# Masked keys written straight from PSUM, two first LayerNorm sums on ScalarE, and a replayed instruction plan with other constants

## The chip, the cores and the metric

The kernel runs on one core of a Trainium2 chip. The core has a matrix engine (TensorE, PE in the profile, with its weight loads as PEld), a vector engine (VectorE, DVE), a scalar engine (ScalarE, ACT), a small general engine (GpSimd, POOL) and a queue engine that issues most transfers (SyncE, SP). Each runs its own list of instructions in order and waits on semaphores for the others. Matmul results land in PSUM, which is divided into eight banks; everything else lies in SBUF.

The metric is the device time of one execution in microseconds (us). The time before is 551.91 us, the median of five runs (551.07 to 553.73).

## The reference

Two layers, each a sliding-window attention and a gated feed-forward block, over a sequence of 2048 with 512 features. Both layers use the same weights.

```python
def _A_ref(x, wqkv, wo):
    H = 32; Dh = D // H; W = 256
    qkv = ... (x @ wqkv) ...                      # q, k, v: 32 heads of 16
    scores = jnp.einsum("bhqd,bhkd->bhqk", q, k) * (Dh ** -0.5)
    mask = (idx[:, None] - idx[None, :] >= 0) & (idx[:, None] - idx[None, :] < W)
    p = _softmax(jnp.where(mask[None, None], scores, -1e9), axis=-1)
    o = jnp.einsum("bhqk,bhkd->bhqd", p, v)
    return ... o ... @ wo

def _B_ref(x, w_gate, w_up, w_down):              # 512 -> 1792 -> 512
    h = _sigmoid(x @ w_gate) * (x @ w_up)
    return h @ w_down

x = x + _A_ref(_layernorm(x, axis=-1), A_wqkv, A_wo)
x = x + _B_ref(_layernorm(x, axis=-1), B_w_gate, B_w_up, B_w_down)
...
return x
```

The two lines are done twice. LayerNorm has no weights: subtract the mean, divide by the root of the variance plus 1e-5.

## The kernel before

**Tiling.** The sequence is 16 tiles of 128 rows; four tiles make a group. The residual `xsb` stays in SBUF for the whole kernel. Every step of the network is cut into small units, and units of attention, of the projections and of the feed-forward block, of different tiles and both layers, are interleaved on TensorE. A PSUM tile `Sps` of four banks holds the scores of one visit; the other four banks are given to units in turn.

**The units.** For each tile: LayerNorm (`layer_norm`, L489), with the sums on VectorE (L498, L499), the root on GpSimd (L503, L504), the normalisation on VectorE (L520), and a transpose, for the first tiles on TensorE (L532, copied out by the helper at L553 and L555), for the others by a transfer on SP (L544). For each group: four q units (L572) and four k units (L601), and a v unit for each tile (L637). The keys are needed twice, in two copies that have every other 16 rows set to zero, since a head has only 16 features and a row group of TensorE holds two heads. So a k unit copies its bank to `kt` (ScalarE or VectorE), and VectorE then multiplies it with two 0/1 columns, `rms[0]` and `rms[1]`, into the two halves of `kTp` (L615). Then come the scores (visits "A", "R" and "S", L853 to L873), exp on ScalarE from `Sps` into `PTring` or `edge` (L905), the masks on VectorE (L791), the values (L932), a copy to `OTs`, two transposes by transfers with the normalisation of the softmax between them (L951, L986, L987, L959), and the output projection (L723) with its addition to `xsb` (L729). The feed-forward block has gate and up matmuls (L662), tanh on ScalarE (L674; a sigmoid is half of one plus tanh of the half), a multiplication on VectorE (L677), and the down matmuls (L695) with their addition (L704).

**The order.** No loop nest sets the order. A planner (`Plan`, L168) simulates the five engines with a clock of its own while the kernel is being built. It gives each instruction a cost in nanoseconds, each task a priority (a lower number goes first), and, whenever an engine is free in its clock, emits the best task that is ready; `pick` (L1029) does so for TensorE. What comes out is a fixed list for each engine. So a changed cost or priority changes the lists of all engines from that point on, also where no operation changes. Where TensorE has nothing ready in the planner's clock and it is before 85 us, the planner emits four dummy matmuls of the identity (`keep_warm`, L1108, instructions at L1112), which compute nothing that is used. The planner's matmul costs are doubled until `COLD` (L102, L283):

```python
    def matmul(self, mode, ns):
        if self.now < COLD:
            ns *= 2
        if self.mode != mode:
            ns += SWITCH
```

Feed-forward units take two tiles at a time (matmuls 256 wide), and one tile at a time (128 wide) for the first four tiles and the last four (L1285). The functions that the change touches:

Of the kernel before, what the change touches and what calls it, by code (L numbers as in the profile page):

```python
# [13 lines left out]
P = 128  # L14
# [65 lines left out]
def act_ns(n):  # L80
    return 171 + n / 1.2


def dve_ns(n):
    return 152 + n / 0.96
# [15 lines left out]
PE_LATENCY = 180  # L101
COLD = 13600  # L102
SWITCH = 96
# [195 lines left out]
class Net:  # L299
# [189 lines left out]
    def layer_norm(self, key, t, deps, prio):  # L489
# [11 lines left out]
        def root(e):  # L501
            st = box["st"][0]
            nc.gpsimd.tensor_scalar(out=st[:, 9:10], in0=st[:, 7:8], scalar1=1e-5, scalar2=None, op0=ALU.add)  # L503
            nc.gpsimd.tensor_tensor(out=st[:, 8:9], in0=st[:, 9:10], in1=self.nhalf[:], op=ALU.pow)  # L504
# [10 lines left out]
        def apply(e):  # L515
            box["xn"] = b = self.take("xn")
            if key not in self.xnT:
                self.xnT[key] = self.take("xnT")
            st = box["st"][0]
            nc.vector.tensor_scalar(out=b[0][:], in0=self.xsb[:, t, :], scalar1=st[:, 6:7], scalar2=st[:, 8:9],  # L520
                                    op0=ALU.subtract, op1=ALU.mult)

        a = pl.task({"DVE": 910}, stats, deps, prio, lambda: self.has("st"))
        b = pl.task({"POOL": 800}, root, [a.done], prio)
# [68 lines left out]
    def k_unit(self, L, g, cq):  # L593
# [10 lines left out]

        def evac(u):
            box = {}
            u.done.then(lambda: self.used(key, 1))

            def cp(e):
                box["kt"] = self.take("kt")  # L610
                self.copy(e, box["kt"][0][:], self.banks[u.bank][:])

            def split(e):
                for i in range(2):
                    nc.vector.tensor_scalar(out=self.kTp[gi % 2][:, cq, :, i, :], in0=box["kt"][0][:].rearrange("p (t k) -> p t k", k=P),  # L615
                                            scalar1=self.rms[i][:, 0:1], scalar2=None, op0=ALU.mult)

            a = pl.task({"ACT": act_ns(TGW), "DVE": dve_ns(TGW)}, cp, [u.done], 2, lambda: self.has("kt"))
            b = pl.task({"DVE": 620}, split, [a.done], 2, port=True)
            b.done.then(lambda: (self.give(box["kt"]), self.k_ready[L, g, cq].fire()))  # L620
            return a.done
# [3 lines left out]
        if gi >= 2:  # L625
            needs.append(self.seen[divmod(4 * (gi - 2) + 3, NT)])
        u = Unit(("k", L, g, cq), steps, needs, False, evac)
        if by_tile:
# [61 lines left out]
    def down_unit(self, L, t, t0, n, chunks):  # L690
# [12 lines left out]
        def evac(u):  # L703
# [3 lines left out]
            if L == 0:  # L707
                self.layer_norm(("p", 1, t // NBG), t, [d.done], 3)
            else:
                dst = self.out[0, t * P:(t + 1) * P, :].rearrange("(z k) d -> z k d", z=2)  # L710
                for z in range(2):
                    pl.dma(450, HP * D * 2, lambda z=z: nc.sync.dma_start(out=dst[z], in_=self.xsb[z:P:2, t, :]), [d.done])
# [6 lines left out]
    def oproj_unit(self, L, t, b):  # L719
# [7 lines left out]
        def evac(u):  # L727
            u.done.then(lambda: self.give(b))
            d = pl.task({"DVE": dve_ns(D)}, lambda e: nc.vector.tensor_tensor(  # L729
                out=self.xsb[:, t, :], in0=self.xsb[:, t, :], in1=self.banks[u.bank][:], op=ALU.add), [u.done], 1)  # L730
            self.layer_norm(("g", L, t // NBG), t, [d.done], 1 if L * NT + t < 4 else 2)
            return d.done
# [33 lines left out]
    def visit_exp(self, s):  # L766
# [14 lines left out]
        def job(h, what):  # L781
# [6 lines left out]
            if what == "m2":  # L788
# [3 lines left out]
                out=r, in0=r, in1=m.to_broadcast([P, 16, HP]), op=ALU.mult), [x.done, self.has_mask],  # L792
                {"m0": 2, "e0": 2, "e1": 6, "m2": 6}[what], port=True).done
            for hh in ((0, 1) if what[0] == "e" else (h,)):
# [38 lines left out]
    def scores(self, L, t, kind, i):  # L833
# [5 lines left out]
        if kind == "A":  # L839
# [9 lines left out]
            for e in range(2):  # L849
                for k, pos, n in runs:  # L850
                    q0, o = t * P + (k + 1) * HP, e * w + pos * HP
                    for m in range(4):
                        nc.tensor.matmul(self.sps[:, m, o:o + n * HP], lhsT=kTp[32 * m:32 * m + 32, i, tt, e, :],  # L853
                                         rhs=self.qT[32 * m:32 * m + 32, i, q0:q0 + n * HP],
                                         start=True, stop=True, tile_position=(32 * m, 0))
            return pl.count(8 * len(runs)) or 220
        if kind == "R":
            zs = range(2 if t + 2 < NT else 1)
            for z in zs:
                for cq in range(NCQ):  # L860
                    q0, o = t * P + 5 * z * HP, (z * NCQ + cq) * HP
                    for m in range(4):
# [3 lines left out]
                                         start=True, stop=True, tile_position=(32 * m, 0))  # L866
            return pl.count(16 * len(zs)) or 122 * len(zs)
        for cq in range(NCQ):
# [38 lines left out]
    def values(self, L, t, half, bank):  # L907
# [7 lines left out]
        for col in range(4):  # L915
# [10 lines left out]
            for k, (where, Va, p) in enumerate(parts):  # L926
# [8 lines left out]
                pl.count(4)  # L935
        return n * 56

    def after_values(self, L, t, half, bank, done):
# [21 lines left out]

        a = pl.task({"DVE": dve_ns(512), "ACT": act_ns(512)}, move, [done], 0 if early else 1, lambda: "OTs" in box or self.has("OTs"))
        box[half] = a.done
# [3 lines left out]
        if self.by_pe(L, t):  # L966
            self.turn_by_pe(L, t, box)
            return
        b = pl.dma(1800, 262144, turn, [box[0], box[1]], 0 if early else 1)
        b.can = lambda: self.has("Oq")  # L970
        b.done.then(lambda: self.give(box["OTs"]))
        c = pl.task({"DVE": 960}, norm, [b.done], 0 if early else 2, lambda: self.has("On"), port=True)
        c.done.then(lambda: (self.give(box["Oq"]), self.give(box["Rt"])))
        d = pl.dma(1190, 131072, turn2, [c.done], 0 if early else 1)
        d.can = lambda: self.has("OnT")
# [258 lines left out]
    def go(self, *srcs):  # L1234
# [47 lines left out]
        for L in range(2):  # L1282
            t0 = 0
            while t0 < NT:
                k = 1 if L * NT + t0 < 4 or L * NT + t0 >= 2 * NT - 4 else 2  # L1285
                m = FC * k // 2
# [59 lines left out]
```

## Time and profile before

| what | value |
|---|---|
| five runs | 551.07 to 553.73 us, median 551.91 |
| profiled execution | 551.91 us, of which its span is 550.2 us |
| POOL busy, share of the span | 61.9 us, 11% |
| exp on ScalarE (L905), `PTring` and `edge` | 154 instructions, 282.5 us |
| gate and up matmuls, 256 wide / 128 wide | 1344 / 896 |
| down, output projection, q, k, v matmuls, 512 wide | 448, 128, 124, 124, 128 |
| dummy matmuls (L1112) | 84, from 1.4 to 58.1 us |
| first scores (L853) on TensorE | 13.79 us |

The page gives the busy time of each engine, and groups of equal instructions with their count, their sum and the mean time of one. Matmuls are pipelined: one of 128 columns is shown with 219 ns, but the next starts 56 ns later, so a cost on TensorE is read from the distance of starts in the timeline and not from the length of one instruction. "Idle before, releaser" says how long an engine had nothing to do ahead of an instruction, and what ended it; "issue" stands for waits that the profile can't put down to another engine or transfer. The timeline gives start, duration, engine, line, operation and tiles, with equal neighbours merged into one row (x12).

### The profile page before, as it was taken

To read this page: it belongs to the slowest core of one execution; us is meant where nothing else is said; L and a number is where in the kernel's file an instruction comes from. 1 tells how busy PE (TensorE), PEld (TensorE's weight loads), DVE (VectorE), ACT (ScalarE), POOL (GpSimd) and SP (SyncE) were. 2 spreads that over 40 slices of the span, in tenths; PEclk is the share of its full clock that TensorE was granted. 3 is DMA by queue.
4 is the path that set the end of the run, shared out by engine and by line. 5 is a ranking of instruction groups with operands and counts; after the bars stand their busy time and mean duration, and the time that the engine had idled before them with its cause. 6 is when DMAs were issued, how large, how long until landed. Compare 5 with 4: busy or idle time off the path is not lost.

```text
span 550.2 us, 24339 instructions
## 1 busy us (share of the span) xinstructions
PE 526.9 (96%) x10953; PEld 355.3 (65%) x11052; DVE 413.1 (75%) x901; ACT 398.4 (72%) x464; POOL 61.9 (11%) x145
## 2 busy tenths in 40 slices
PE   7999999999999999999999999999999999989996
PEld 6547757757667566666566664666756766667883
DVE  6999898697799698789675795867766677756442
ACT  3998889889889788677687875878768777643320
POOL 5212110020011120002010120100000000000000
PEclk9999999999999999999999999999999999999999
DMA  8694423153223332125201252013520142222000
GB/s 275 210 177 141 61 47 57 31 64 70 43 58 63 71 42 61 32 56 94 49 14 30 52 89 62 17 37 69 90 70 13 41 85 57 50 50 54 17 21 29
DMA packets 97016, 36.43 MB, mean 66 GB/s; under 512 B 79248, under 2 KB 96912, under 8 KB 96912
## 3 DMA queue, kind: packets, MB, share of 16 engines
q1 hardware_dynamic: 95040, 33.04, 28.3%
q8 instruction: 86, 1.41, 1.0%
q10 hardware_dynamic: 1872, 1.84, 1.0%
q14 instruction: 18, 0.15, 0.1%
HBM read 9.70 MB, written 2.10 MB: 21 GB/s over the span
## 4 chain that ended last, share of the span: by engine, by line
PE 88%; issue 3%; DMA 3%; ACT 3%; DVE 2%; SPq 0%; ACTq 0%; DVEq 0%
PE bank L662 34%; PE bank L695 16%; PE bank L932 8%; PE Sps L853 7%; PE bank L601 5%; PE bank L572 5%; PE bank L723 5%; PE bank L637 5%; DMA OnT<-On 2%; ACT PTring L905 2%; PE Sps L863 2%; DMA xnT<-xn 1%; DVE st L498 0%; DVE xn L520 0%; PE bank L532 0%
## 5 line engine op out<-in xcount | busy, mean ns | idle before, releaser
L905 ACT ACTIVATE PTring<-Sps 128x2048 bf16<-128x2048 f32 (+1 forms) x122 | 225.8, 1851 | 49.5 <-PE Sps L853 47.1
L662 PE MATMUL bank<-xnT,wu 128*128 128x256 bf16 (+1 forms) x1120 | 139.8, 251 | 0.7 <-issue 0.7
L662 PE MATMUL bank<-xnT,wg 128*128 128x256 bf16 (+1 forms) x1120 | 139.0, 252 | 0.2
L677 DVE SCALAR_TENSOR_TENSOR hT<-th,bank 128x256 bf16<-128x256 bf16 x224 | 87.8, 414 | 40.8 <-ACT th L674 39.8
L674 ACT ACTIVATE th<-bank 128x256 bf16<-128x256 f32 x224 | 81.0, 385 | 51.0 <-PE bank L662 48.1
L695 PE MATMUL bank<-wd,hT 128*128 128x512 bf16 x395 | 104.5, 379 | 3.3 <-issue 1.4
L662 PEld LDWEIGHTS <-wg 128*128 128x128 bf16 x1120 | 90.4, 98 | 26.5 <-issue 2.2
L662 PEld LDWEIGHTS <-wu 128*128 128x128 bf16 x1120 | 92.0, 98 | 12.3 <-issue 1.6
L503 POOL TENSOR_SCALAR st<-st 128x1 f32<-128x1 f32 x64 | 19.4, 303 | 442.3 <-DVE st L499 442.3
L791 DVE TENSOR_TENSOR PTring<-PTring,mask 128x1024 bf16<-128x1024 bf16 x64 | 44.0, 687 | 30.8 <-ACT PTring L905 30.5
L905 ACT ACTIVATE edge<-Sps 128x2048 bf16<-128x2048 f32 (+1 forms) x32 | 56.7, 1773 | 12.8 <-PE Sps L863 12.8
L695 PEld LDWEIGHTS <-hT 128*128 128x128 bf16 x448 | 40.8, 98 | 32.1 <-issue 0.6
L932 PE MATMUL bank<-PTring,Vaug 128*32 128x64 bf16 (+1 forms) x2880 | 52.1, 203 | 0.5 <-issue 0.5
L853 PE MATMUL Sps<-qT,kTp 32*128 32x64 bf16 (+3 forms) x1856 | 48.0, 218 | 3.0 <-ACT PTring L905 1.2
L932 PEld LDWEIGHTS <-Vaug 128*32 128x32 bf16 x2880 | 43.9, 97 | 10.5 <-issue 7.3
L853 PEld LDWEIGHTS <-kTp 32*128 32x128 bf16 x1856 | 25.0, 92 | 39.3 <-issue 37.3
L932 PE MATMUL bank<-edge,Vl 128*32 128x64 bf16 x1024 | 44.8, 193 | 1.8 <-issue 1.8
L791 DVE TENSOR_TENSOR edge<-edge,maske 128x1024 bf16<-128x1024 bf16 x60 | 40.5, 684 | 4.9 <-ACT edge L905 4.8
L498 DVE BATCH_NORM_STATS2 st<-xsb 128x6 f32<-128x512 bf16 x64 | 43.7, 683 | 0.4
L555 DVE CAST OTs<-bank 128x512 bf16<-128x512 f32 x51 | 37.2, 730 | 8.0 <-PE bank L932 7.3
L932 PE MATMUL bank<-edge,Vh 128*32 128x64 bf16 x896 | 40.9, 193 | 0.0
L504 POOL TENSOR_TENSOR st<-st,nhalf 128x1 f32<-128x1 f32 x64 | 39.0, 610 | 5.3
(73 smaller groups left out, 525.3 us busy)
## 6 DMA issues: line engine op xcount, KB each, us to landing
Vl<-Vaug SPq DMA_DIRECT2D x32, 68.0 KB, 2.3
out_dram<-xsb SPq DMA_DIRECT2D x32, 64.0 KB, 1.9
Vh<-Vaug SPq DMA_DIRECT2D x28, 68.0 KB, 2.5
wg<-in_B_w_gate_dram SPq DMA_DIRECT2D x2, 896.0 KB, 11.8
wu<-in_B_w_up_dram SPq DMA_DIRECT2D x2, 896.0 KB, 9.3
wd<-in_B_w_down_dram SPq DMA_DIRECT2D x7, 256.0 KB, 4.1
wq<-in_A_wqkv_dram ACTq DMA_DIRECT2D x3, 512.0 KB, 6.3
xsb<-in_A_x_dram SPq DMA_DIRECT2D x6, 256.0 KB, 5.5
```

Of the source, the lines that this page charges most:

```text
L498: nc.vector.bn_stats(out=st[:, 0:6], in_=self.xsb[:, t, :])
L504: nc.gpsimd.tensor_tensor(out=st[:, 8:9], in0=st[:, 9:10], in1=self.nhalf[:], op=ALU.pow)
L555: self.nc.vector.tensor_copy(out=out, in_=in_)
L572: return [(mm_ns(w), lambda kt=kt, o=o: nc.tensor.matmul(self.banks[bank][:, o:o + w], lhsT=self.wq[:, kt, cq * P:cq * P + P], rhs=self.xn ...
L662: return [(mm_ns(w), lambda i=i, j=j, fc=fc, wt=wt, kt=kt: nc.tensor.matmul(pt[:, i, j, :], lhsT=wt[:, kt, fc * P:(fc + 1) * P], rhs=self. ...
L674: nc.scalar.activation(out=box["th"][0][:], in_=pt[:, 0, :], func=AF.Tanh, scale=0.5)
L677: nc.vector.scalar_tensor_tensor(out=self.hT[:, chunk, :], in0=box["th"][0][:], scalar=1.0, in1=pt[:, 1, :], op0=ALU.add, op1=ALU.mult)
L695: nc.tensor.matmul(self.banks[bank][:], lhsT=self.hT[:, c, o:o + P], rhs=self.wd[:, fc, :], start=fc == 0, stop=fc == FC - 1)
L791: done = pl.task({"DVE": dve_bf_ns(1024)}, lambda e: nc.vector.tensor_tensor(out=r, in0=r, in1=m.to_broadcast([P, 16, HP]), op=ALU.mult), ...
L853: nc.tensor.matmul(self.sps[:, m, o:o + n * HP], lhsT=kTp[32 * m:32 * m + 32, i, tt, e, :], rhs=self.qT[32 * m:32 * m + 32, i, q0:q0 + n * ...
L905: nc.scalar.activation(out=out, in_=src, func=AF.Exp, scale=scale)
L932: nc.tensor.matmul(o, lhsT=Va[:, c0:c0 + 32], rhs=p(h), start=k == 0 or t == 0, stop=k == len(parts) - 1 or t == 0, tile_position=(0, 32 * g))
```

## The change

- `k_unit`: for the first group of the first layer (four units), no copy to `kt`. Two tasks read the bank in PSUM, each multiplies it with one 0/1 column and writes one half of `kTp`. Each can go to ScalarE (an activation with a scale per partition) or to VectorE; the planner chooses. The bank is free when both are done. The other units keep the old way.
- `layer_norm`: for the third and fourth tile of the first group, the sums are taken on ScalarE. An Identity activation with scale -1/512 accumulates the negative mean, a Square activation with that as its bias accumulates the sum of squares; both write their elementwise result to a part of `edge` that isn't in use yet. GpSimd multiplies by 1/512 and adds 1e-5 in the same instruction as before, and the normalisation adds instead of subtracting.
- Constants of the plan: `COLD`, the costs of scores and values, and priorities of LayerNorm, masks, the copy to `OTs` and the transposes of attention.
- `go`: the last four tiles are taken in pairs too.

```diff
-COLD = 13600
+COLD = 6800
...
         def root(e):
             st = box["st"][0]
-            nc.gpsimd.tensor_scalar(out=st[:, 9:10], in0=st[:, 7:8], scalar1=1e-5, scalar2=None, op0=ALU.add)
+            if by_act:
+                nc.gpsimd.tensor_scalar(out=st[:, 9:10], in0=st[:, 7:8], scalar1=1.0 / D, scalar2=1e-5, op0=ALU.mult, op1=ALU.add)
+            else:
+                nc.gpsimd.tensor_scalar(out=st[:, 9:10], in0=st[:, 7:8], scalar1=1e-5, scalar2=None, op0=ALU.add)
...
             nc.vector.tensor_scalar(out=b[0][:], in0=self.xsb[:, t, :], scalar1=st[:, 6:7], scalar2=st[:, 8:9],
-                                    op0=ALU.subtract, op1=ALU.mult)
-
-        a = pl.task({"DVE": 910}, stats, deps, prio, lambda: self.has("st"))
+                                    op0=ALU.add if by_act else ALU.subtract, op1=ALU.mult)
+
+        def stats2(e):
+
+            box["st"] = b = self.take("st")
+            st, junk = b[0], self.edge[:, 5, 0:D // HP, :].rearrange("p m q -> p (m q)")
+            nc.scalar.activation(out=junk, in_=self.xsb[:, t, :], func=AF.Identity, scale=-1.0 / D, accum_out=st[:, 6:7])
+            nc.scalar.activation(out=junk, in_=self.xsb[:, t, :], func=AF.Square, bias=st[:, 6:7], accum_out=st[:, 7:8])
+
+        by_act = key == ("p", 0, 0) and t >= NBG - 2
+        if by_act:
+            a = pl.task({"ACT": 1350}, stats2, deps, prio, lambda: self.has("st"))
+        else:
+            a = pl.task({"DVE": 910}, stats, deps, prio, lambda: self.has("st"))
...
         def evac(u):
+            u.done.then(lambda: self.used(key, 1))
+
+            def part(e, i):
+                src = self.banks[u.bank][:].rearrange("p (t k) -> p t k", k=P)
+                dst = self.kTp[gi % 2][:, cq, :, i, :]
+                if e == "ACT":
+                    nc.scalar.activation(out=dst, in_=src, func=AF.Identity, scale=self.rms[i][:, 0:1])
+                else:
+                    nc.vector.tensor_scalar(out=dst, in0=src, scalar1=self.rms[i][:, 0:1], scalar2=None, op0=ALU.mult)
+
+            parts = [pl.task({"ACT": act_ns(TGW), "DVE": dve_ns(TGW)}, lambda e, i=i: part(e, i), [u.done], 2).done
+                     for i in range(2)]
+            both = Event()
+            when_all(parts, both.fire)
+            both.then(self.k_ready[L, g, cq].fire)
+            return both
+
+        def evac_by_copy(u):
...
-        u = Unit(("k", L, g, cq), steps, needs, False, evac)
+        u = Unit(("k", L, g, cq), steps, needs, False, evac if gi < 1 else evac_by_copy)
...
             if L == 0:
-                self.layer_norm(("p", 1, t // NBG), t, [d.done], 3)
+                self.layer_norm(("p", 1, t // NBG), t, [d.done], 4)
...
-            self.layer_norm(("g", L, t // NBG), t, [d.done], 1 if L * NT + t < 4 else 2)
+            self.layer_norm(("g", L, t // NBG), t, [d.done], 1 if L * NT + t < 4 else 3)
...
-                {"m0": 2, "e0": 2, "e1": 6, "m2": 6}[what], port=True).done
+                {"m0": 2, "e0": 2, "e1": 5, "m2": 5}[what], port=True).done
...
-            return pl.count(8 * len(runs)) or 220
+            return pl.count(8 * len(runs)) or 232
...
-            return pl.count(16 * len(zs)) or 122 * len(zs)
+            return pl.count(16 * len(zs)) or 125 * len(zs)
...
-        return n * 56
+        return n * 62 + 15
...
-        a = pl.task({"DVE": dve_ns(512), "ACT": act_ns(512)}, move, [done], 0 if early else 1, lambda: "OTs" in box or self.has("OTs"))
+        a = pl.task({"DVE": dve_ns(512), "ACT": act_ns(512)}, move, [done], 0 if early else 0, lambda: "OTs" in box or self.has("OTs"))
...
-        b = pl.dma(1800, 262144, turn, [box[0], box[1]], 0 if early else 1)
+        b = pl.dma(1800, 262144, turn, [box[0], box[1]], 0 if early else 2)
...
-        c = pl.task({"DVE": 960}, norm, [b.done], 0 if early else 2, lambda: self.has("On"), port=True)
+        c = pl.task({"DVE": 960}, norm, [b.done], 0 if early else 3, lambda: self.has("On"), port=True)
...
-        d = pl.dma(1190, 131072, turn2, [c.done], 0 if early else 1)
+        d = pl.dma(1190, 131072, turn2, [c.done], 0 if early else 2)
...
-                k = 1 if L * NT + t0 < 4 or L * NT + t0 >= 2 * NT - 4 else 2
+                k = 1 if L * NT + t0 < 4 or L * NT + t0 >= 2 * NT - 0 else 2
```

## The prediction

> **What bounds the kernel now.** First the page's busy times, then TensorE's own waits, then the front's timeline.
>
> ```profile
> PE 526.9 (96%) x10953; PEld 355.3 (65%) x11052; DVE 413.1 (75%) x901; ACT 398.4 (72%) x464; POOL 61.9 (11%) x145
> ```
> ```profile
> PE bank L932 <- issue: 2.4, 3, 1.8
> ...
> PE Sps L853 <- ACT PTring L905: 1.2, 4, 0.4
> PE bank L723 <- DMA OnT<-On: 1.1, 3, 0.5
> ```
> TensorE is busy for 526.9 of 550.2 us. Its idle 23.3 us lie, by the busy times of stretches, 3.7 us before 12 us, 4.1 us after 540 us and 15.5 us spread between; of these the waits for another engine or a transfer are short, 1.2 us for exp the largest sum. So the time is the moment at which TensorE gets its first real work, plus what its list holds, plus some stalls. A change pays only through one of these three.
>
> ```profile
> 1.44 5.53 PE L1112 MATMUL bank<-ident 128*128 128x128 bf16 x56 [1.44 <-POOL ident L438]
> ...
> 8.63 0.56 POOL L504 TENSOR_TENSOR st<-st,nhalf 128x1 f32<-128x1 f32 x1
> ...
> 8.87 1.56 ACT L553 COPY xnT<-bank 128x512 bf16<-128x512 bf16 x3 [3.56 <-PE bank L532]
> ...
> 10.19 0.40 DVE L520 TENSOR_SCALAR xn<-xsb,st 128x512 bf16<-128x512 bf16 x1
> ...
> 10.65 0.40 PE L532 MATMUL bank<-ident,xn 128*128 128x128 bf16 x4 [0.54 <-DVE xn L520]
> ...
> 11.08 0.59 ACT L553 COPY xnT<-bank 128x512 bf16<-128x512 bf16 x1 [0.65 <-PE bank L532]
> 11.72 0.38 PE L601 MATMUL bank<-xnT,wq 128*128 128x128 bf16 x4 [0.23 <-ACT xnT L553]
> ...
> 11.94 1.06 PE L572 MATMUL bank<-xnT,wq 128*128 128x128 bf16 x16
> 12.14 0.59 ACT L553 CAST kt<-bank 128x512 bf16<-128x512 f32 x1 [0.47 <-PE bank L601]
> 12.76 0.61 DVE L615 TENSOR_SCALAR kTp<-kt,rm 128x512 bf16<-128x512 bf16 x2 [2.17 <-ACT kt L553]
> ...
> 13.03 0.59 ACT L553 CAST qT<-bank 128x512 bf16<-128x512 f32 x1 [0.31 <-PE bank L572]
> ...
> 13.79 0.41 PE L853 MATMUL Sps<-qT,kTp 32*128 32x128 bf16 x24
> ```
> The front is a chain through the fourth tile's normalisation (10.19), its transpose, its copy, the last k and q matmuls, and the copy of q (ends 13.62). The masked keys are done at 13.37, earlier than q. From the normalisation's start to the first scores it takes 3.60 us; the fourth tile decides.
>
> **The change, part by part.**
>
> *LayerNorm sums on ScalarE.* VectorE loses two pairs of L498 and L499, 0.81 us each (starts 6.39, 7.20, 8.00). In the new order the eight small mask instructions (8.94 to 10.19: 1.25 us) stand right behind tile 2's sums on VectorE, ahead of all four normalisations, so the first of these starts at 6.39 + 1.25 = 7.64 instead of 8.00. On ScalarE four instructions of 128x512 stand between the table load (ends 5.30) and the first copy, where ScalarE idles 3.56 us. Their kind is not in this trace. Lower bound: the copies, three in 1.56, 0.52 each, 2.1 us in all. Upper: 0.59 for a copy alone, 0.24 for the longest pause that ScalarE makes on its own account between two copies (before 16.98), and 0.18 for taking a statistic out, as L499 does: 1.0 each, 4.0 us. They end at 7.4 to 9.3. Their data is no limit: VectorE reads tile 2 at 6.39 without a wait, and by the issue rows (issued by 1.5, 4.1 us to landing) it is there at 5.6. The roots go through POOL in a queue of 0.85 us each (5.77, 6.62, 7.48, 8.32); POOL then ends the fourth at 9.19, as before, or at 0.9 behind ScalarE, 10.2. The fourth normalisation, which today waits for its place behind the masks, starts at 9.25 or 10.2 instead of 10.19. Its copy on ScalarE queues behind three others, of which the first starts at 8.51 at the earliest, so not before 10.07; a start at 9.25 needs it at 9.25 + 0.89 = 10.14, which fits. I take 9.25, nearest to the copy rows, whose shapes are the same: **-0.94 us**, bounds 0 and -1.05.
>
> *Keys straight from PSUM.* A k unit costs today a copy and two splits.
>
> ```profile
> L615 DVE TENSOR_SCALAR kTp<-kt,rm 128x512 bf16<-128x512 bf16 x64 | 19.2, 346 | 9.8 <-ACT kt L553 9.7
> ...
> L553 ACT CAST kt<-bank 128x512 bf16<-128x512 f32 x20 | 11.7, 593 | 2.6 <-PE bank L601 2.4 <-ACT kt L553 0.2
> ...
> L555 DVE CAST kt<-bank 128x512 bf16<-128x512 f32 x12 | 8.1, 685 | 0.2
> ```
> Now it is two reads of the bank. In the built order five of the eight parts are ScalarE's, three VectorE's. ScalarE: four copies of 0.593 become five parts, +0.6 us. VectorE: four pairs of splits (0.61 for a pair at 12.76) become three parts of 0.685, -0.4 us. For the first scores that is nothing: q covers it, by 13.62 - 13.37 = 0.25 us, and the chain above doesn't contain the keys. If q were earlier, it would pay up to 12.76 + 0.61 - 12.14 - 0.69 = 0.5 us. Queued behind the ScalarE parts are q's copy (13.03; a part that starts at 12.14 ends before it) and the first exps: at worst the 0.6 us reach them, at best nothing. I take nothing: what reaches them shows as waits on TensorE that the plan's dummies fill, and those are priced below.
>
> The Trainium skill's page "VectorE: DVE Perf Modes", section "Rules for kernel authors", speaks against this edit: on a matmul's output either accept the slow rate or copy out first if several operations follow. The rows agree on the rate (685 against 346 ns); by the rule the engines' sum wouldn't fall, and by the rows it doesn't (+0.2 us over four units). Its page "ScalarE: Activation LUTs", section "What ACT_TABLE_LOAD costs", adds about 93 ns for a per-partition pointer operand, which the five parts and two of the sums have; an estimate by it is 0.65 us more of ScalarE, which no row here shows.
>
> *The plan.* All orders are replayed with other costs. The old plan doubles every matmul's time until 13.6 us, the new one until 6.8; in the trace the first 56 take 99 ns each (5.53 us), while the eight at 10.88 take 0.61 us, 56 ns each behind the first, so the new one is nearer, and nothing on the chip changes by it but the order. In the built program the warm-up matmuls (L1112) go from 84 to 124. In front of the first scores they go from 60 to 76, where TensorE waits anyway; cover: the front's idle 3.7 us. Behind it they go from 24 to 48. Of the old ones, the four at 36.77 stand ahead of a transpose whose input came at 36.70, and hide; the four at 32.30 stand ahead of scores whose exp had ended at 32.06, and cost. So a group costs between 0 and 4 x 56 ns; 24 more cost 0 to 1.34 us. I take half, **+0.67 us**.
>
> *The last four tiles in pairs.*
> ```profile
> 495.57 0.60 PE L662 MATMUL bank<-xnT,wg 128*128 128x256 bf16 x4
> 496.00 0.60 PE L662 MATMUL bank<-xnT,wu 128*128 128x256 bf16 x4
> ```
> ```profile
> 511.34 0.61 PE L662 MATMUL bank<-xnT,wg 128*128 128x128 bf16 x8
> ...
> 511.78 0.61 PE L662 MATMUL bank<-xnT,wu 128*128 128x128 bf16 x8
> ```
> Starts lie 0.435 us apart for four 256-wide and 0.445 for eight 128-wide: 109 and 56 ns each. 448 narrow ones become 224 wide ones: 25.1 to 24.4, **-0.67 us**, on the path. The last 28 down matmuls, the last add and the store stay as they are.
>
> *Waits in the middle.* Scores have one tile (Sps), so between two visits TensorE needs other work for exp's 1.88 us and two hand-overs; the tightest round trips in the trace are 2.2 to 2.3 us. I filled the gaps of both orders with 56, 109 and 216 ns (30 down matmuls in 6.64 us from 539.44) a matmul. Before, seven gaps are under 2.30 and lack 2.07 us in all, which agrees with the 1.2 us waited for exp plus 0.7 put down to issue at L853. After, again seven, lacking 0.98. **-1.09 us**, bounds 0 and -1.9. SP's queue: between the two transposes of an attention tile other issues grow from 49 to 59 over the 30 tiles, at 1.2 us each; the tiles with six or seven between have 13.5 us and more of TensorE work before their output projection, against about 8 us needed (cast 0.73, landing 3.2, normalising 1.04, landing 2.5, hand-overs). So nothing, bounds in the rival below.
>
> Sum: -0.94 + 0.67 - 0.67 - 1.09 = -2.03 us. The profiled run took 551.91 us, 1.71 around its span of 550.2, and it is itself the median of the five (551.07 to 553.73). **Forecast 549.9 us.**
>
> **Rivals.** *The front's gain is eaten.* All 48 extra dummies cost and exp waits stay: -0.94 + 1.34 - 0.67 = -0.27, 551.6 us. For: from 20 to 60 us VectorE (36.3 of 40) and ScalarE (35.6) are nearly as full as TensorE (38.6), so an earlier start may only wait earlier. Against: VectorE sheds 1.6 us of sums just before.
>
> *The sums don't come early.* ScalarE holds the copies up and the first scores stay at 13.79: 550.8 us. For: the kind is unmeasured. Against: 3.56 us of room.
>
> *Slower: the attention transposes come late.* In the new plan they rank with or behind other tasks on SP, so ten more issues stand inside the 30 turns. If each 1.2 us of them reached the output projection that is 12 us; they cost 0.4 us a tile on average. TensorE waited for OnT on 7 of 32 tiles. If seven tiles again have no slack and each meets half an issue, 0.6 x 7 = 4.2 us: 554.1. It decides from 3.7 us of new waits at L723 on (2.03 + 1.65). For: the 59, and seven tiles still have under 11 us of cover. Against: those seven have at most two other issues between.
>
> **How the numbers follow.** Forecast (faster): 0.62, with its own range 547.0 to 550.2. First and second rival: 0.17 together. Slower: 0.21, including long single stalls like the 1.8 us at L932, which a new order draws anew. 0.3% is 1.65 us, about what this kernel's runs tell apart. Low end: front -1.05, tail -0.67, exp -1.9 and that 1.8 us stall gone, minus 5.4: 546.5. High end: front 0, tail -0.67, exp 0, dummies +1.34 and one more such stall, plus 2.5: 554.4.
>
> **What would show it.** First scores at 12.7 to 13.2 us; POOL's fourth root ending near 9.2; L1112 behind the front without idle TensorE around it; wide matmuls at 109 ns to the end; TensorE's waits for exp under 1 us. Wrong if waits at L723 or for xnT pass 3.7 us, or if the first scores are earlier and the 60 us mark isn't.

## The result, and the profile after

The changed kernel takes 553.87 us (median of 27 runs) beside 551.6 us before: a ratio of 1.0042, 95% interval 1.003 to 1.0054. It is slower, by 2.3 us, where the forecast said 2.0 us faster. The profiled execution took 553.66 us, its span is 551.9 us. Of `h_keys` and `h_early` below, one run each was over 5% longer with TensorE at 0.91 and 0.89 of full speed, and is left out of their medians and ratios.

TensorE's row of the page, and the rows of the view of waits (what was waited for; sum in us, times, longest) that answer to those shown of before:

```profile
PE 530.4 (96%) x10776; PEld 356.3 (65%) x10868; DVE 414.8 (75%) x896; ACT 401.6 (73%) x469; POOL 64.6 (12%) x145
```
```profile
PE bank L546 <- DVE xn L523: 1.9, 2, 1.0
...
PE bank L964 <- issue: 1.4, 1, 1.4
PE Sps L885 <- ACT PTring L937: 1.2, 1, 1.2
PE bank L755 <- DMA OnT<-On: 1.0, 2, 0.8
```

TensorE is no less busy (530.4 of 551.9 us). The waits for exp (L885, which was L853) again sum to 1.2 us, now in one piece; those for OnT (L755, was L723) stay at 1.0. So the slower rival, late attention transposes, isn't what happened. What differs most is the front; the timeline after (start, duration, engine, line):

```profile
5.82 1.28 ACT L530 ACT_TABLE_LOAD   x1 [5.82 <-DMA xsb<-in_A_x_dram]
...
7.11 0.63 ACT L530 ACTIVATE edge<-xsb 128x512 bf16<-128x512 bf16 x1
...
7.65 0.19 ACT L530 ACTIVATION_READ_ACCUMULATOR edge<-xsb 128x1 f32 x1
7.87 0.72 ACT L531 ACTIVATE edge<-xsb,st 128x512 bf16<-128x512 bf16 x1
...
10.10 0.19 ACT L531 ACTIVATION_READ_ACCUMULATOR edge<-xsb,st 128x1 f32 x1
...
10.19 1.54 ACT L567 COPY xnT<-bank 128x512 bf16<-128x512 bf16 x3
...
10.65 0.55 POOL L507 TENSOR_TENSOR st<-st,nhalf 128x1 f32<-128x1 f32 x1
...
11.19 1.06 PE L1144 MATMUL bank<-ident 128*128 128x128 bf16 x8
11.23 0.41 DVE L523 TENSOR_SCALAR xn<-xsb,st 128x512 bf16<-128x512 bf16 x1 [1.19 <-ACT xnT L567]
...
13.32 1.06 PE L1144 MATMUL bank<-ident 128*128 128x128 bf16 x8
14.17 0.43 PE L615 MATMUL bank<-xnT,wq 128*128 128x128 bf16 x4
...
14.64 0.69 ACT L626 ACTIVATE kTp<-bank,rm 128x512 bf16<-128x512 f32 x1 [1.34 <-PE bank L615]
15.36 0.75 DVE L628 TENSOR_SCALAR kTp<-bank,rm 128x512 bf16<-128x512 f32 x1 [3.71 <-ACT kTp L626]
...
16.29 0.41 PE L885 MATMUL Sps<-qT,kTp 32*128 32x128 bf16 x24
```

The first scores start at 16.29 us instead of 13.79: 2.50 us late, where 0.94 us early was forecast. Read it from the top. The table load starts at 5.82, behind the arrival of the tile; the copies' load before ended at 5.30, and this one ends at 7.10. Each sum is two instructions, the activation (0.63 or 0.72) and a separate read of the accumulator (0.19). They end at 10.29, and ScalarE's first copy waits behind them until 10.19 (8.87 before). The fourth root ends at 11.20 on GpSimd, its normalisation starts at 11.23 (10.19 before). And one more thing: eight dummies at 11.19 take 1.06 us, where eight matmuls of that shape took 0.61 before (at 10.88). The view by stretches shows the clock (columns: busy us of PE, PEld, DVE, ACT, POOL; then PEclk, the granted clock as a share; DMA share; GB/s). First the kernel before, then after:

```profile
11.00:14.00 3.00, 2.72 (x52) 1.99 (x54) 1.22 (x3) 1.86 (x4) 0.00 (x0) 1.00 1.08 366
```
```profile
8.00:10.00 2.00, 1.07 (x16) 0.90 (x16) 0.71 (x3) 1.94 (x5) 0.74 (x2) 1.00 1.10 356
10.00:11.00 1.00, 0.59 (x7) 0.47 (x8) 0.04 (x1) 1.00 (x4) 0.54 (x2) 0.91 1.11 352
11.00:14.00 3.00, 3.00 (x31) 3.00 (x30) 0.41 (x1) 1.32 (x3) 0.20 (x1) 0.50 1.07 365
```

TensorE is busy for 1.07 of 2 us from 8 to 10, and from 11 to 14 its clock is 0.50; before, it was busy for 1.54 of these 2 us and kept 1.00. The busy share of these 2 us alone doesn't decide it: `h_early`, below, is busy for 1.13 of them and keeps 1.00. Nor does every run have it: seven of the changed kernel's runs have a mean clock of at least 0.999, where 3.4 us at half speed would take off 0.003, and their median is 552.36 us. In this execution the dummies at 13.32 hold up k matmuls whose input had been ready since 13.30, until 14.17.

From the first scores to TensorE's last start it is 545.70 - 13.79 = 531.9 us before and 547.42 - 16.29 = 531.1 after: 0.8 us less. With +2.50 that is +1.7, and the two profiled executions differ by 553.66 - 551.91 = 1.75. One execution of each doesn't show a gain behind the first scores, though: the profiled executions of `after0`, `a_warm` and `a_early` below, which have the changed kernel's lists but for a few instructions in front, take 532.1, 532.5 and 534.0 us for the same stretch. The timed runs lose some tenths more than 1.75. Their granted clock averages 0.9959, that of the kernel before 0.9965 to 0.998 in the four later sets of runs, and among the runs of after 0.001 of clock goes with 0.43 us.

### The profile page after: what moved, and what is told of

It reads as the page before. It is cut to its first block, busy times and chain, and to the rows that moved or that the text cites. A ratio compares the mean times of both kernels' runs of the same rounds, so it can differ in the third digit from the quotient of the medians.

```text
span 551.9 us, 23997 instructions
## 1 busy us (share of the span) xinstructions
PE 530.4 (96%) x10776; PEld 356.3 (65%) x10868; DVE 414.8 (75%) x896; ACT 401.6 (73%) x469; POOL 64.6 (12%) x145
## 4 chain that ended last, share of the span: by engine, by line
PE 87%; DVE 4%; ACT 3%; issue 3%; DMA 2%; SPq 0%; ACTq 0%; DVEq 0%
PE bank L694 33%; PE bank L727 16%; PE bank L964 8%; PE Sps L885 6%; PE bank L755 5%; PE bank L615 5%; PE bank L669 5%; PE bank L586 5%; PE Sps L895 2%; DMA OnT<-On 2%; ACT PTring L937 1%; PE bank L1144 1%; DMA xsb<-in_A_x_dram 1%; DVE PTring L823 1%; DVE xn L523 1%
## 5 line engine op out<-in xcount | busy, mean ns | idle before, releaser
L694 PEld LDWEIGHTS <-wg 128*128 128x128 bf16 x1008 | 86.8, 98 | 26.9 <-issue 2.3
L694 PEld LDWEIGHTS <-wu 128*128 128x128 bf16 x1008 | 89.6, 98 | 12.7 <-issue 0.7
L506 POOL TENSOR_SCALAR st<-st 128x1 f32<-128x1 f32 x62 | 17.8, 287 | 437.7 <-DVE st L499 437.7
L885 PE MATMUL Sps<-qT,kTp 32*128 32x64 bf16 (+3 forms) x1856 | 47.8, 218 | 1.6 <-ACT PTring L937 1.2
L885 PEld LDWEIGHTS <-kTp 32*128 32x128 bf16 x1856 | 24.6, 93 | 36.8 <-issue 34.9
L507 POOL TENSOR_TENSOR st<-st,nhalf 128x1 f32<-128x1 f32 x64 | 42.6, 666 | 5.3
L498 DVE BATCH_NORM_STATS2 st<-xsb 128x6 f32<-128x512 bf16 x62 | 42.4, 684 | 0.6
```

Source lines behind the costliest of these rows:

```text
L498: nc.vector.bn_stats(out=st[:, 0:6], in_=self.xsb[:, t, :])
L694: return [(mm_ns(w), lambda i=i, j=j, fc=fc, wt=wt, kt=kt: nc.tensor.matmul(pt[:, i, j, :], lhsT=wt[:, kt, fc * P:(fc + 1) * P], rhs=self. ...
```

## The experiments

Each ratio is to the kernel before on the same chip in the same set of runs, with its 95% interval. The medians of the kernel before in the four sets are 553.18 us (runs that begin with `a_`), 552.06 (`f_` and `after0`), 552.28 (`h_sums`, `h_keys`, `t_pairs`, `n_222`) and 553.32 (the last four); the second and third set ran on the same chip.

### What the front costs, with the changed kernel's lists

Three kernels keep the new plan. In `a_early`, a one-column activation ahead of the sums:

```diff
+            if t == NBG - 2:
+                nc.scalar.activation(out=b[0][:, 9:10], in_=self.nhalf[:], func=AF.Identity)
```

> The changed kernel, all lists the same, but for one ScalarE activation of a single column (from a constant) ahead of the sums, so that the table load hangs on that constant and not on the x transfer. Late-sums theory: the load starts at 4.0 instead of 5.82, the sums end at 8.5 to 8.9 instead of 10.29, the first scores come 1.5 to 1.9 us earlier plus what the clock gives, 13.5 to 14.8, time down by 1.5 to 2.5 us. Clock theory (the half clock from 10.96 to 14.37 us is the larger part): if the clock still drops, under 1 us gained. Plan theory: no gain in the time.

Measured: 552.92 us, 1.0004 (0.9989 to 1.002); first scores 13.77. Timeline:

```profile
4.02 1.28 ACT L530 ACT_TABLE_LOAD   x1 [4.02 <-DMA xsb<-in_A_x_dram]
5.31 0.20 ACT L530 ACTIVATE st<-nhalf 128x1 f32<-128x1 f32 x1
...
5.99 0.63 ACT L532 ACTIVATE edge<-xsb 128x512 bf16<-128x512 bf16 x1 [0.47 <-DMA xsb<-in_A_x_dram]
...
8.97 0.19 ACT L533 ACTIVATION_READ_ACCUMULATOR edge<-xsb,st 128x1 f32 x1
...
10.10 0.41 DVE L523 TENSOR_SCALAR xn<-xsb,st 128x512 bf16<-128x512 bf16 x1 [1.19 <-POOL st L507]
...
13.77 0.41 PE L887 MATMUL Sps<-qT,kTp 32*128 32x128 bf16 x24
```

The load is back at 4.02, the sums run from 5.99 (the first still waits for its tile) to 9.16. One tiny instruction recovers the 2.5 us of the start. But the normalisation starts at 10.10, so the sums don't bring the front forward either. In this execution the head start is still 2.1 us at the last exp (484.9 us, 487.0 in the changed kernel), and then it is lost:

```profile
491.83 0.21 PE L966 MATMUL bank<-PTring,Vaug 128*32 128x64 bf16 x2 [1.98 <-issue]
```

TensorE stops for 2.0 us, its clock is 0.51 from 492.0 to 495.5, and its last start comes at 547.76, 0.34 later than in the changed kernel. What the start is worth is therefore read from the timed runs: `a_early` is 0.39% below `a_warm`, the next kernel, which ran beside it and starts its scores 1.80 us later.

In `a_warm` the load stays late and the gaps of TensorE are filled:

```diff
-        for i in range(4):
+        for i in range(12 if 6900 < pl.now < 7000 else 18 if 7800 < pl.now < 7900 else 4):
```

> The changed kernel, all lists the same, but for 22 more dummy matmuls in the two gaps in which TensorE idles at 7.2 and 9.2 us. Clock theory: the clock stays full, eight dummies take 0.6 us instead of 1.06, first scores at 15.0 to 15.4 instead of 16.29, time 1 us lower and a smaller spread of the runs. Late-sums theory: the copies still start at 10.19, so the first scores stay behind 15 us and at most 1.2 us are gained.

Measured: 555.02 us, 1.0043 (1.0024 to 1.0062); the clock stays at 1.00.

```profile
6.48 1.28 ACT L530 ACT_TABLE_LOAD   x1 [6.48 <-DMA xsb<-in_A_x_dram]
...
7.78 0.63 ACT L530 ACTIVATE edge<-xsb 128x512 bf16<-128x512 bf16 x1
...
15.57 0.41 PE L885 MATMUL Sps<-qT,kTp 32*128 32x128 bf16 x24
```

From the first sum to the first scores: 15.57 - 7.78 = 7.8 us, and 13.77 - 5.99 = 7.8 in `a_early`, but 16.29 - 7.11 = 9.2 in the changed kernel. So of its 2.50 us, 1.1 are the later first sum (7.11 - 5.99: the load's 1.28 behind the tile, which came 0.17 earlier) and 1.4 are the half clock. The end didn't gain: in `a_warm`'s execution the load came 0.66 us later still, and a wait of 1.7 us for OnT stood at 118 us. `a_both` has both edits (of the dummies only the first 8):

> The early table load and eight more dummies in the first gap together. If the two causes add up: first scores at 13.4 to 13.9 us, full clock, time 551.0 to 551.8, the time of the kernel before. Plan theory: still 553.

Measured: 554.05 us, 1.0018 (0.9999 to 1.0037), first scores 14.98.

```profile
7.20 0.63 ACT L532 ACTIVATE edge<-xsb 128x512 bf16<-128x512 bf16 x1 [1.69 <-DMA xsb<-in_A_x_dram]
```

Not better than `a_early`. The load is early again (4.01), but in this execution the tile itself came only at 7.20, and 14.98 - 7.20 = 7.8 us once more. So the early load takes away the 1.28 us behind the tile, and not the wait for the tile, which the sums on ScalarE pass on to the copies. The tile's arrival moves from one execution to the next (5.82, 6.48 and 7.20 us in these).

### The sums taken away, and each part alone

`a_vec` is the changed kernel with the sums back on VectorE; the planner draws the order anew:

```diff
-        by_act = key == ("p", 0, 0) and t >= NBG - 2
+        by_act = False
```

> The changed kernel with the sums of all four first tiles on VectorE again; all else of the change stays and the plan is replayed. Late-sums theory (the front lost 2.5 us because four sums of 0.8 us, behind a table load that waits for x, stand ahead of the first copies on ScalarE): first scores at 13.3 to 13.9 us instead of 16.29, table load again near 4.0, full clock throughout, time 1.5 to 3 us under the changed kernel. Plan theory (the new order of the middle is what costs): first scores earlier, but the time stays within 1 us of the changed kernel.

Measured: 557.09 us, 1.0087 (1.0051 to 1.0123). The front is repaired (13.64), and the kernel is slower than with the fault in it. So the front isn't all, and the next set took the parts one at a time, each with the order that the planner draws for it: `f_sums` and `f_keys` are the kernel before with that edit only, `f_plan` is the changed kernel without both (constants, priorities, pairs), `after0` the changed kernel again.

> The kernel before with the sums of tiles 2 and 3 on ScalarE as its only edit (old constants, old keys, last four tiles one by one). Late-sums theory: the table load waits for the tile again and the sums stand ahead of the copies, so the first scores start at 15.5 to 16.3 us instead of 13.79, and what follows keeps its length (531.9 us from the first scores to TensorE's last start): +1.7 to +2.5 us, ratio 1.003 to 1.005. Clock theory: the same, and the granted clock shows half speed somewhere between 8 and 15 us. Plan theory (the lists behind the front are what costs): the late start is absorbed by waits that the old order had anyway, ratio under 1.002.

> The kernel before with the keys straight from PSUM as its only edit. By the forecast it is worth nothing: first scores at 13.3 to 13.8 us, ratio 0.999 to 1.001. Late-sums theory says the same. Plan theory: the replayed order behind the front differs though the edit only touches four units, and may cost or gain up to 2 us by stalls that are drawn anew, ratio 0.996 to 1.004; the ramp from the first to the sixth score column then takes over 16.5 us instead of 15.8.

> The changed kernel without its two data edits: the constants, the priorities and the last four tiles in pairs stay. Late-sums theory: the front is the old one, first scores at 13.3 to 13.9 us, and the pairs and shorter waits in the middle pay 0.7 to 1.8 us: ratio 0.996 to 0.999. Plan theory: first scores as early, but a ratio of 1.003 to 1.009, with stalls of over 1.5 us in back-to-back value units and exp waits in the ramp.

> The changed kernel itself, run beside the others so that all are compared on one chip. Any theory: ratio 1.002 to 1.006, first scores at 16.3 us; the clock theory adds that the half clock between 10.8 and 14.2 us is there again.

| kernel | median us | ratio (interval) | first scores |
|---|---|---|---|
| `f_sums` | 558.38 | 1.0105 (1.0076 to 1.0134) | 15.88 |
| `f_keys` | 557.06 | 1.0078 (1.0053 to 1.0102) | 13.81 |
| `f_plan` | 559.19 | 1.0122 (1.0092 to 1.0152) | 13.87 |
| `after0` | 556.60 | 1.0081 (1.0055 to 1.0106) | 16.00 |

Each part by itself costs about as much as all three together, or more, also the two that leave the front alone. `after0` is slower here than in its first runs; its granted clock averages 0.993, against 0.998 for the kernel before beside it; at the 0.43 us above that is an estimated 1.9 of the 4.5 us that it loses here. So ratios of different chips can differ by 0.4% for the same kernel. What the parts share isn't work but a redrawn order, and the next set tests whether that is the cause. `f_plan`'s timeline shows one place where such an order fails (ScalarE's copy to `Vaug` is first):

```profile
30.29 1.08 ACT L567 CAST Vaug<-bank 128x512 bf16<-128x512 f32 x2 [4.16 <-DMA Vl<-Vaug]
30.93 1.02 PE L586 MATMUL bank<-xnT,wq 128*128 128x512 bf16 x4 [2.49 <-ACT Vaug L567]
31.25 1.90 ACT L937 ACTIVATE PTring<-Sps 128x2048 bf16<-128x2048 f32 x1
...
33.20 0.61 PE L895 MATMUL Sps<-qT,kTp 32*128 32x64 bf16 x32 [1.24 <-ACT PTring L937]
```

ScalarE idles 4.16 us for the transfer that reads `Vaug` for `Vl`, because the copy stands next in its list; TensorE waits 2.5 us for the bank that the copy holds, and the exp queued behind it makes TensorE wait 1.2 us more. From 33.0 to 36.4 us TensorE's clock is then 0.50.

### The same edits with the old order held

Here the planner isn't told of the edit, so the lists stay the old ones. `h_sums` emits the four activations where the planner believes it emits VectorE's sums; `h_keys` emits both halves where it believes it emits the copy, and nothing at the splits:

```diff
             st = b[0]
+            if by_act:
...
+                nc.scalar.activation(out=junk, in_=self.xsb[:, t, :], func=AF.Identity, scale=-1.0 / D, accum_out=st[:, 6:7])
+                nc.scalar.activation(out=junk, in_=self.xsb[:, t, :], func=AF.Square, bias=st[:, 6:7], accum_out=st[:, 7:8])
+                return
```
```diff
-                self.copy(e, box["kt"][0][:], self.banks[u.bank][:])
+                part(e, 0)
+                if gi < 1:
+                    part("DVE", 1)
```

`t_pairs` has only the last four tiles in pairs, and `n_222` one planner constant changed by 1%:

```diff
-                k = 1 if L * NT + t0 < 4 or L * NT + t0 >= 2 * NT - 4 else 2
+                k = 1 if L * NT + t0 < 4 or L * NT + t0 >= 2 * NT else 2
```
```diff
-            return pl.count(8 * len(runs)) or 220
+            return pl.count(8 * len(runs)) or 222
```

> The sums of tiles 2 and 3 on ScalarE, but the planner is not told: TensorE's, GpSimd's and SyncE's lists are the old ones row for row, VectorE's and ScalarE's differ only by the moved sums. Order theory (an edit costs its own microseconds in front, the rest of its price is the redrawn order): first scores at 15.5 to 16.3 us, and the ratio is what that start gives, 1.002 to 1.005, well under the 1.0105 of the same edit with its own order. Rival (the sums cost it all, the order nothing): ratio 1.008 to 1.012 again.

> The keys of the first group straight from PSUM, but the planner is not told: TensorE's, GpSimd's and SyncE's lists are the old ones row for row; half 0 stands where the copy stood, half 1 on VectorE right with it. Order theory: ratio 0.998 to 1.002, as forecast for this edit, against the 1.0078 of the same edit with its own order. Rival (reading PSUM twice is what costs): 1.005 to 1.008 again, with the loss inside the first 30 us.

> The kernel before with only the last four tiles in pairs; every list is the old one up to the tail, about 495 us. By the forecast -0.67 us, 256-wide matmuls every 109 ns to the end: ratio 0.998 to 0.9995. Rival (wider tiles make TensorE wait for the activations of the last pair, tanh and product of 256 columns instead of 128): ratio 1.001 to 1.003, with new waits of gate and up or of the down matmuls behind 530 us. Order theory has nothing against the gain, since no order before 495 us changes.

> The kernel before with one constant of the plan changed: the planner counts a score column as 222 ns instead of 220. The same instructions, in another order from TensorE's row 1294 of 22106 on. Order theory (the order before is a favourable one, a redrawn order is worse whatever redraws it): ratio 1.003 to 1.012, first scores at 13.8 us as before. Rival (an order drawn by a neutral cause is as good as the old one): ratio 0.998 to 1.002.

| kernel | median us | ratio (interval) | with its own order |
|---|---|---|---|
| `h_sums` | 554.16 | 1.0040 (1.0027 to 1.0053) | 1.0105 |
| `h_keys` | 553.23 | 1.0022 (1.0006 to 1.0039) | 1.0078 |
| `t_pairs` | 551.87 | 0.9991 (0.9975 to 1.0007) | |
| `n_222` | 555.63 | 1.0074 (1.0048 to 1.0101) | |

With the order held, the two edits cost 0.65% and 0.56% less, 3 to 3.6 us; the two sets ran on one chip, but not side by side. And an order redrawn by nothing but a constant costs 0.74%, more than either held edit in the same set. So the order theory is borne out: by these numbers the larger part of the price of each single edit is the new order. `h_keys` stays at +0.2% where nothing was expected; in its profiled execution TensorE waited 1.2 us in front for the transfer of wq, which the edit doesn't touch, ran at a clock of 0.50 from 11 to 14 us, and started the scores at 15.45; whether the timed runs have that is open.

Three waits of `n_222`, where before has 1.1 us for OnT (L723) and, put down to issue, 0.7 at L662 and 2.4 at L932; then four stretches, columns as above:

```profile
PE bank L662 <- issue: 3.2, 5, 1.4
PE bank L723 <- DMA OnT<-On: 2.6, 3, 0.9
...
PE bank L932 <- issue: 2.0, 1, 2.0
```
```profile
233.00:235.00 2.00, 2.00 (x155) 1.36 (x155) 1.92 (x4) 1.12 (x1) 0.00 (x0) 1.00 0.03 8
235.00:237.30 2.30, 0.28 (x35) 0.17 (x22) 0.00 (x0) 1.38 (x2) 0.78 (x2) 1.00 0.00 0
237.30:238.60 1.30, 1.30 (x14) 0.62 (x13) 0.79 (x2) 0.00 (x0) 0.00 (x0) 1.00 0.05 13
238.60:242.00 3.40, 3.40 (x21) 1.72 (x20) 1.98 (x4) 1.89 (x2) 0.00 (x0) 0.51 0.15 30
```

OnT costs 1.5 us more, issue at both lines together 2.1 more. And in the row of value matmuls from 234 us on TensorE stands for 2.0 us, the clock then falls to 0.51 for 3.4 us, which is 1.7 us more. Twenty more dummies are in its list. This execution took 558.41 us, the timed median is 555.63, so not all of it is in every run.

`t_pairs` did what was forecast, its interval also allows nothing. Its last rows of TensorE:

```profile
538.56 0.60 PE L662 MATMUL bank<-xnT,wg 128*128 128x256 bf16 x4
539.00 0.60 PE L662 MATMUL bank<-xnT,wu 128*128 128x256 bf16 x4
539.43 6.64 PE L695 MATMUL bank<-wd,hT 128*128 128x512 bf16 x30
```

Starts 0.44 us apart for four 256-wide matmuls, 110 ns each, to the end, and no new wait. From the last scores to TensorE's last start it is 57.8 us, before 58.3: -0.5 us.

### The forecast's chain, with the masks moved instead of the sums

`m_late` is before with one held move: VectorE's eight small mask instructions are emitted after the fourth tile's normalisation instead of ahead of it.

```diff
         def mask2(e):
+            self.mask2 = small
+
+        def small():
...
                                     op0=ALU.subtract, op1=ALU.mult)
+            if key == ("p", 0, 0) and t == NBG - 1:
+                self.mask2()
```

`m_pairs` adds the pairs to it, `h_early` is `h_sums` with the one-column activation of `a_early`, and `n_57` changes another constant, the 56 ns of a value matmul to 57.

> The kernel before with one held move: the eight small mask instructions of VectorE stand behind the fourth tile's normalisation instead of ahead of it; every other row of every list is the old one. The forecast's chain (the fourth tile's normalisation decides the first scores, and it waits for its place behind the masks): normalisation at 9.25 instead of 10.19, first scores at 12.8 to 13.3 instead of 13.79, and with the order held the start is handed on: ratio 0.998 to 0.9995. Rival (another wait stands right behind, the wq transfer or ScalarE's queue of copies): first scores at 13.5 or later, ratio 0.9995 to 1.001.

> The same held move and the last four tiles in pairs: candidate for a kernel that beats both. Order theory: the two gains add, -0.5 to -0.9 and -0.4 to -0.7 us, ratio 0.997 to 0.9985. Rival (the start's gain is lost at a later wait): ratio 0.9985 to 1.0005, as for the pairs alone.

> The sums on ScalarE with the old order held, and a one-column activation in front of them so that the table load need not wait for the tile. Late-table theory: first scores at 13.6 to 14.6 us instead of the 18.2 with the load waiting, ratio 0.999 to 1.002 against 1.004. Rival (the sums' own length holds the copies up even so): first scores at 15 us or later, ratio 1.002 to 1.004.

> The kernel before with another constant of the plan changed by a little: a value matmul counts as 57 ns instead of 56. Order theory: ratio 1.003 to 1.012 again, by other waits than the 222 ns order; first scores at 13.8. Rival (the 222 ns order was an unlucky one, the mean of redrawn orders is no worse than the old order): ratio 0.998 to 1.002.

| kernel | median us | ratio (interval) | first scores |
|---|---|---|---|
| `m_late` | 551.66 | 0.9973 (0.9953 to 0.9994) | 13.08 |
| `m_pairs` | 552.56 | 0.9991 (0.9967 to 1.0015) | 13.38 |
| `h_early` | 553.34 | 0.9992 (0.9965 to 1.0019) | 13.72 |
| `n_57` | 553.45 | 1.0021 (1.0003 to 1.0039) | 13.81 |

The kernel before beside them: 553.32 us. `m_late`'s front:

```profile
8.62 0.56 POOL L507 TENSOR_TENSOR st<-st,nhalf 128x1 f32<-128x1 f32 x1
...
9.22 0.41 DVE L523 TENSOR_SCALAR xn<-xsb,st 128x512 bf16<-128x512 bf16 x1 [0.20 <-POOL st L507]
...
9.54 0.34 DVE L477 TENSOR_REDUCE odd<-ident 128x1 f32<-128x64 bf16 x2
...
13.08 0.41 PE L858 MATMUL Sps<-qT,kTp 32*128 32x128 bf16 x24
```

The root ends at 9.18 and the normalisation starts at 9.22; the forecast had 9.25. The first scores come 0.71 us earlier. `m_late` is faster than the kernel before beside it, by an interval that ends just under 1, and by its ratio faster than the changed one. Among runs with a granted clock of at least 0.9985 the medians are 551.49 and 552.08, 0.6 us apart, which agrees with the start; the rest goes with the clock, 0.9988 on average against 0.9965. `m_pairs`, which has the same move, isn't shown to be faster than the kernel before, nor the pairs on top to add anything; the intervals overlap.

`h_sums` (timeline, then a stretch), then `h_early`:

```profile
7.37 1.28 ACT L500 ACT_TABLE_LOAD   x1 [7.37 <-DMA xsb<-in_A_x_dram]
...
8.66 0.63 ACT L500 ACTIVATE edge<-xsb 128x512 bf16<-128x512 bf16 x1
...
18.20 0.41 PE L862 MATMUL Sps<-qT,kTp 32*128 32x128 bf16 x24
```
```profile
11.00:14.00 3.00, 2.25 (x20) 1.93 (x21) 1.95 (x10) 2.35 (x6) 0.90 (x3) 0.50 1.08 365
```
```profile
4.02 1.28 ACT L500 ACT_TABLE_LOAD   x1 [4.02 <-DMA xsb<-in_A_x_dram]
...
5.97 0.63 ACT L502 ACTIVATE edge<-xsb 128x512 bf16<-128x512 bf16 x1 [0.46 <-DMA xsb<-in_A_x_dram]
...
13.72 0.41 PE L864 MATMUL Sps<-qT,kTp 32*128 32x128 bf16 x24
```

In the first the load waits for the tile until 7.37 in this execution and the first scores come at 18.20, in the second at 13.72. Of these 4.5 us, 1.4 are a tile that came later (7.37 against 5.97), 1.3 the load behind it, and 1.8 lie between the first sum and the scores, where the clock was 0.50 from 11 to 16 us. With the load early the sums cost nothing that the timed runs can tell, and gain nothing. `n_57` says that a redrawn order is not always as dear: +0.2% and +0.7% for two neutral causes, a gain in neither.

## Why the prediction was wrong

*LayerNorm sums on ScalarE* is the step that failed: -0.94 us forecast, +2.50 measured, outside its bounds of -1.05 and 0. It took the table load as given, "between the table load (ends 5.30) and the first copy". But the load stands ahead of the first activation and, as built, waits for that activation's transfer: 5.82 instead of 4.02. In the bounds the sums began at 5.30, and their data was taken to be no limit, there at 5.6. But tile 2 arrives between 5.63 and 7.37 in the eight profiled executions that sum it on ScalarE; with the load early the sums begin at 5.97, 5.99 and 7.20. The two sums of two tiles, four activations, then take 3.2 us, inside the 2.1 to 4.0; the lower bound was taken for the shape's sake, and the reading of the accumulator (0.19 each) and 0.63 to 0.72 for the activation are nearer to the middle. The forecast's end of 7.4 to 9.3 became 10.29 (9.16 without the late load). So with the load early the normalisation starts at 10.10 and the gain is nothing (13.77), where 9.25 was taken. And no term allowed for the clock: half speed in front costs 1.4 us in the profiled execution, though not in every run. The chain itself was right, as `m_late` shows: normalising the fourth tile at 9.22 brings the scores 0.71 us forward, of the 0.94 claimed. It only needed the masks moved, not the sums.

*Keys straight from PSUM*: the parts take 0.69 us on ScalarE, 0.75 on VectorE (0.685 taken). The forecast let the keys end 0.25 us ahead of q. In the changed kernel VectorE's part starts only when ScalarE's has ended (15.36; 14.64 + 0.69), and the profile names ScalarE's write to `kTp` as what released it. One behind the other they end at 16.11, and q's copy at 16.12, so the cover is gone. The Trainium skill's page "ScalarE: Activation LUTs", section "What ACT_TABLE_LOAD costs", gives about 93 ns for a pointer operand; the row agrees, 0.69 against 0.59 for a copy. Nothing was forecast; +0.2% with the order held, up to 0.39% by the interval.

*The last four tiles in pairs*: -0.67 forecast, -0.5 us in the profile and -0.4 (-1.4 to +0.4) in the runs. Right, as far as that tells.

*The plan* and *Waits in the middle* can't be told apart in the changed kernel: together with the pairs they were to give -1.09, and the five profiled executions with the changed kernel's lists, or nearly those, take 0.8 us less to 2.1 us more than before from the first scores on. So a gain isn't shown, and exp waits stayed at 1.2 us, where they were to halve. No run prices the +0.67 for dummies by itself. The way of reckoning failed too: gaps counted from two lists with fixed durations left out that any new order moves waits for OnT, `Vaug`, and the long stops in value rows. The runs price a redrawn order at +0.2 to +0.7% (1.2 to 4.1 us) for neutral causes, and 3 us for the sums and the keys, as large as all terms of the forecast. That the forecast's high end, 554.4, lies above the result is luck: it is made of dummies and one more stall, with a front that loses nothing.

*The rivals*: the front's gain was not eaten, it never came. The second rival, by which ScalarE holds the copies up and the scores stay at 13.79, comes nearest: so it is with the load early (13.77), and as built it was 2.5 us worse. Of the attention transposes nothing is seen in the changed kernel (1.0 us of waits for OnT, 1.1 before), so the slower rival had the sign and the wrong place.

## What to carry over

An instruction that becomes the first on its engine may pull setup work, like a table load, behind its own data; give the setup something that is ready at once. In a kernel whose order is planned ahead, measure an edit with the order held and then with the order redrawn: the two prices differ, and the second can be the larger one. A wait for a place in a list was mended here by moving what stood ahead.

## What the hardware showed that was not expected

The granted clock fell to one half without any long pause of TensorE: in the changed kernel after gaps of 0.9, 0.95 and 0.3 us within 3.4 us, in `n_222` after one stop of 2.0 us, and both times for 3.4 us. The Trainium skill's page "TensorE: Matmul & The Clock Gate", section "Why this matters for your kernels", advises against idle gaps of more than about 3 us; in these rows less was enough. Not always: the stop of 1.8 us at 493 us in the kernel before left the clock at 1.00. What decides isn't shown.

In dense rows of value matmuls (in `n_222` a group of four starts every 30 to 60 ns) TensorE stops for 1.4 to 2.4 us at 231 to 235 or 490 to 499 us in most kernels, before too. In all sixteen such stops of over 1.3 us, in 14 of the 18 profiled executions, a 16 KB packet on the instruction queue starts between 1.0 us before the stop and 0.03 us after its beginning, takes 0.9 to 1.5 us, and the matmuls go on 1.2 to 1.6 us after its end; an execution has 86 such packets, one in 6.4 us. That the list of instructions runs dry there is argued from this, not shown; no run changed it.
